# The last rows of w4: from 512-column to 256-column matmuls, smaller last pieces, and a result stored in two halves

## The chip, the cores and the metric

The kernel runs on one core of one Trainium2 chip. The metric is the time of one execution in device microseconds; lower is better. Beside it stands the span, which is the part of the execution that the profiled instructions cover.

## The reference, cut to what matters

One token is decoded by an attention block over a cache of 65,536 keys and, on the same normalised input, by a mixer block; both are added to the input.

```
xn  = layernorm(x)                                     # x: 1 x 1024
q   = (xn @ wq), 32 heads of 128                       # 4 groups of 8 heads share a K and V cache
p   = softmax(q . k_cache / sqrt(128))                 # 65536 keys a group
A   = (p @ v_cache) as one row of 4096 @ wo            # wo: 4096 x 1024
h   = gelu(layernorm(xn) @ w1), shifted along the sequence (length 1)
x1  = xn + h_shifted @ w2
B   = x1 + gelu(layernorm(x1) @ w3) @ w4               # w4: 3584 x 1024
out = x + A + B
```

The sequence has length 1, so the shifted columns of `h` are zeros. All inputs and the output are bf16. The caches are 2 x 4 x 65536 x 128 values, 134 MB, and the weights are another 36 MB.

## The kernel before

Everything is streamed once through three buffers of 64 KB per partition (`slot0` to `slot2`), in the order of the list `stream` (L285): wq, w3, w1 and w2, then a K tile and a V tile for each of eight units (`u`: four groups, two halves of the keys), then wo, then w4. Every load is issued on SyncE's queue by `load` (L288); a buffer's next load is issued by `freed` (L311) when the matmuls that read the buffer are done, so that three loads are in the queue or under way at most. w4 alone is loaded in pieces (`W4_PIECES`, L19): 8, 12, 5, 2 and 1 rows, where a row is what one of the 128 partitions holds for one of 28 steps `c`, 1024 values or 2 KB. Each piece has a semaphore of its own, and the first matmul that reads a piece waits for it.

For each unit, `scores` transposes the K tile in place on VectorE and multiplies it with the queries on TensorE; `maxima`, `weights` and `values` follow. `group_rows` (L509) closes a group and leaves its part of the attention's output, as columns, in `oT`.

The end of the kernel, which the change touches, runs after the last group:

- L540: VectorE computes `o`, the sum of the terms that come from the input row, from `x_halves`. That buffer holds the input row in two halves of 512, on partitions 0 and 32.
- L544 to L550: 32 rows of wo and then the first 20 rows of w4 are multiplied by `row_acc` (L342): two matmuls per row, each 512 columns wide, on two of the four column strips of TensorE. They add up in the PSUM tile `psB`, where the attention's wo product and the w2 product meet. Each such matmul has a weight load of its own.
- L552: VectorE adds `psB` and `o` into `sums` (in the buffer `og`).
- L554: `narrow_rows` multiplies the last `NARROW` = 8 rows of w4 by four matmuls each, 256 columns wide, on all four strips, into the PSUM tiles `pm0` and `pm1`. After the first `AHEAD` = 5 of them, two fp32 matmuls (`mm32`, with the selection matrix `pick`) add `sums` into the same tiles; the 3 remaining rows follow.
- L568 to L571: ScalarE casts `pm0`, VectorE casts `pm1`, each into one half of `out_t` (the buffer of `x_halves`), and ScalarE issues one store of 2 KB, from two partitions, when both casts are done.
- L580 to L587: ScalarE clears the semaphores, and SyncE waits for the store.

The order on each engine is the order in which the program records the operations; `Program.plan` (L124) derives the waits from the regions that they read and write, and TensorE's and SyncE's own instructions are taken to run in order. Since a helper records every operation, most operations carry one of a few line numbers: VectorE, ScalarE and GpSimd have L82, matmuls L106 (weight loads L102), fp32 matmuls L116, loads L89 and stores L93.

Of the kernel before, what the change touches and what calls it, by code (L numbers as in the profile page):

```python
# [14 lines left out]
P = 128  # L15
ROW = 32768
SUBS = 4
SETS = 4
W4_PIECES = (8, 12, 5, 2, 1)  # L19
NARROW = 8  # L20
AHEAD = 5

WIDTH = {F32: 4, BF16: 2}

# [182 lines left out]
def kernel(  # L207
# [14 lines left out]
    nc = tc.nc  # L222
    D = A_x.shape[-1]
# [7 lines left out]
    FC = F // P  # L231
    UKEYS = P * ROW // DH
    assert DH == P and HQ // HKV == 8 and HKV == 4 and D == 1024 and F == 3584 and S == 1
    assert SK == 2 * UKEYS and sum(W4_PIECES) == FC
    NB = 2
# [3 lines left out]
    COLS = (P, 32)  # L239

    prog = Program(nc)
    pe, dve, act, pool = prog, prog.dve, prog.act, prog.pool

    def sb(name, shape, dtype=F32):
        return nc.alloc_sbuf_tensor(name, list(shape), dtype)

    def ps(name, shape):
        return nc.alloc_psum_tensor(name, list(shape), F32)
# [4 lines left out]
    x_row = sb("x_row", [32, D], BF16)  # L253
# [4 lines left out]
    x_halves = sb("x_halves", [64, 512], BF16)  # L258
    qdiag = sb("qdiag", [P, LEAD + 4 * P], BF16)
    g_col = sb("g_col", [P, 1], BF16)  # L260
# [9 lines left out]
    hT = sb("hT", [P, FC], BF16)  # L270
    oT = sb("oT", [P, 32], BF16)
    ol = sb("ol", [P, DH + 1])
    pick = sb("pick", [64, 2, 32])
# [3 lines left out]
    pm = [ps(f"pm{i}", [P, 512]) for i in range(2)]  # L277
# [8 lines left out]
    tiles = {it: slots[i % 3] for i, it in enumerate(stream)}  # L286

    def load(it):  # L288
        t = tiles[it]
        if it == "wq":  # L290
            prog.load("sp", t[:], A_wq.rearrange("(p c) n -> p (c n)", c=DC))
        elif it == "w3":
            prog.load("sp", t[:, 0:DC * F], B_w3.rearrange("(p c) f -> p (c f)", c=DC))
        elif it == "w12":
            prog.load("sp", t[:, 0:DC * D], B_w1.rearrange("(p c) n -> p (c n)", c=DC))
            prog.load("sp", t[:, DC * D:2 * DC * D], B_w2.rearrange("(m c) n -> m (c n)", c=DC))
        elif it == "wo":
            prog.load("sp", t[:], A_wo.rearrange("(p j) n -> p (j n)", p=P))
        elif it == "w4":
            w4_v = B_w4.rearrange("(m c) n -> m c n", c=FC)  # L300
            c0 = 0
            for n in W4_PIECES:
                prog.load("sp", t[:, c0 * D:(c0 + n) * D], w4_v[:, c0:c0 + n, :].rearrange("p c n -> p (c n)"))
                c0 += n
        else:
            kind, i = it
            g, b = divmod(i, NB)
            cache = A_k_cache if kind == "K" else A_v_cache
            prog.load("sp", t[:], cache[0, g, b * UKEYS:(b + 1) * UKEYS, :].rearrange("(p ct) d -> p (ct d)", p=P))

    def freed(it):  # L311

        n = stream.index(it) + 3
        if n < len(stream):
            load(stream[n])

    load("wq")
    opening = len(prog.ops)

    dve.memset(x_row[:], 0.0)  # L320
    prog.load("act", x_row[0:1, :], A_x[0, 0:1, :])
    load("w3")
    load("w12")

# [9 lines left out]
    for b in range(2):  # L334
        pool.tensor_copy(
            out=spread[:, 2 * b:2 * b + 2, :].rearrange("p r (a i) -> p r a i", a=4),
            in_=ident_f[:, 64 * b:64 * b + 64].rearrange("p (i r) -> p r i", r=2).unsqueeze(2).to_broadcast([P, 2, 4, 32]))
    pool.memset(x_halves[:], 0.0)
    pool.memset(qdiag[:], 0.0)
    pool.memset(g_col[:], 0.0)  # L340

    def row_acc(j, lhsT, rhs, start=False):  # L342
        return pe.mm(psB[32 * j:32 * j + 32, :], lhsT.to_broadcast([P, 32]), rhs, start, False, (0, 32 * j), COLS)

    x_t = p_sb[:, 0:DC * 32].rearrange("p (c j) -> p c j", j=32)
    for a in range(4):
        dve.transpose(out=x_t[32 * a:32 * a + 32].rearrange("p c j -> p (c j)"),
                      in_=x_row[:, 256 * a:256 * (a + 1)].rearrange("p (i c) -> p c i", c=DC))
    dve.tensor_copy(out=xT[:], in_=x_t[:, :, 0])

    def layernorm(src, tag):
# [31 lines left out]
                    in_=sel8[:].unsqueeze(1).unsqueeze(3).to_broadcast([P, 4, 8, 4]))  # L383
    dve.tensor_copy(out=pick[:],
                    in_=ident_f[0:64, 0:64].rearrange("p (j r) -> p j r", r=32)[:, :, 0:1].to_broadcast([64, 2, 32]))
    dve.tensor_scalar(out=ln_s1[:], in0=rstd1[:], scalar1=1.0, scalar2=None, op0=ALU.add)
    dve.tensor_tensor(out=ln_s2[:], in0=negmean1[:], in1=rstd1[:], op=ALU.mult)
    for j in range(2):
        dve.tensor_copy(out=x_halves[32 * j:32 * j + 1, :], in_=x_row[0:1, 512 * j:512 * (j + 1)])

    def row_matmul(rep, cols, widths):
        for c in range(DC):
# [37 lines left out]
    def compute_w12():  # L430
        wt = tiles["w12"][:, 0:2 * DC * D].rearrange("p (w c n) -> p w c n", w=2, c=DC)
        for c in range(DC):
            for q in range(2):
                pe.mm(sc[0:32, q, :], xn2_rep[:, c, :], wt[:, 0, c, 512 * q:512 * (q + 1)], c == 0, c == DC - 1,
                      (0, 0), COLS)
        h1 = p_sb[0:32, 0:1024].rearrange("p (q n) -> p q n", q=2)
        act.activation(out=h1, in_=sc[0:32, 0:2, :], func=ACTF.Gelu_apprx_tanh)
        for c in range(DC):
            for j in range(2):
                row_acc(j, g_col[:], wt[:, 1, c, 512 * j:512 * (j + 1)], start=(c == 0))  # L440
        freed("w12")

    W = ROW // SETS
# [80 lines left out]
    compute_wq()  # L524
    compute_w3()
    compute_w12()
    for u in range(NU):
        g, b = divmod(u, NB)
# [11 lines left out]
    o = tiles["w4"][0:64, FC * D:FC * D + D].bitcast(F32)  # L540
    dve.tensor_scalar(out=o, in0=x_halves[:], scalar1=ln_s1[0:64, 0:1], scalar2=ln_s2[0:64, 0:1],
                      op0=ALU.mult, op1=ALU.add)

    for j in range(32):  # L544
        for h in range(2):
            row_acc(h, oT[:, j:j + 1], tiles["wo"][:, D * j + 512 * h:D * j + 512 * (h + 1)])
    wt = tiles["w4"]
    for c in range(FC - NARROW):
        for j in range(2):
            row_acc(j, hT[:, c:c + 1], wt[:, D * c + 512 * j:D * c + 512 * (j + 1)])  # L550
    sums = og[0:64, :]
    dve.tensor_tensor(out=sums, in0=psB[0:64, :], in1=o, op=ALU.add)  # L552

    def narrow_rows(lo, hi, start=False):  # L554
        for c in range(lo, hi):
            for h in range(2):
                for j in range(2):
                    q = 2 * h + j
                    pe.mm(pm[h][32 * q:32 * q + 32, 0:256], hT[:, c:c + 1].to_broadcast([P, 32]),
                          wt[:, D * c + 512 * j + 256 * h:D * c + 512 * j + 256 * (h + 1)], start and c == lo, False,  # L560
                          (0, 32 * q), COLS)

    narrow_rows(FC - NARROW, FC - NARROW + AHEAD, start=True)
    for h in range(2):
        pe.mm32(pm[h][64 * h:64 * h + 64, 0:256], pick[:].rearrange("p j r -> p (j r)"),
                sums[:, 256 * h:256 * (h + 1)], False, False, (0, 64 * h))
    narrow_rows(FC - NARROW + AHEAD, FC)
    out_t = x_halves[:].rearrange("p (h n) -> p h n", h=2)  # L568
    act.copy(out=out_t[:, 0, :], in_=pm[0][0:64, 0:256])
    dve.tensor_copy(out=out_t[:, 1, :], in_=pm[1][64:128, 0:256])  # L570
    store = prog.store("act", out[0, 0, :].rearrange("(j n) -> j n", j=2), out_t[31:33].rearrange("p h n -> p (h n)"))  # L571

    prog.plan()
    with tc.tile_critical(sync_engine=mybir.EngineType.Pool, no_gpsimd_drain=True):
# [1 line left out]
    tc.close()  # L576
    tc.compile()
    prog.emit(opening, len(prog.ops))
    nums = sorted(s.num for s in prog.sems if s is not store.sem)
    nc.scalar.sem_clear(range(nums[0], nums[-1] + 1))  # L580
    nc.sync.add_instruction(mybir.InstEventSemaphore(
        name=nc.get_next_instruction_name(), engine=mybir.EngineType.SP, ins=[], outs=[],
        sync_info=mybir.SyncInfo(
            on_wait=[mybir.SyncWait(sync_type="semaphore", id=store.sem.num, ant_name=store.sem.name,
                                    wait_mode="sem-ge-imm", wait_value=16)],
            on_update=[mybir.SyncUpdate(sync_type="semaphore", id=store.sem.num, ant_name=store.sem.name,
                                        update_mode="sem-sub-imm", update_value=16)])))  # L587

# [1 line left out]
_INS = ['A_x', 'A_k_cache', 'A_v_cache', 'A_wq', 'A_wo', 'B_x', 'B_w1', 'B_w2', 'B_w3', 'B_w4']  # L590
# [26 lines left out]
```

## Time and profile before

| | |
|---|---|
| time, median of 3 runs | 400.46 us (400.43 to 400.66) |
| the profiled execution's own time | 400.43 us |
| its span | 399.1 us |
| TensorE, matmuls | 221.0 us busy (55%), 1360 |
| VectorE | 210.2 us busy (53%), 156 |
| ScalarE | 27.6 us busy (7%), 35 |
| bytes moved | 170.03 MB in 3760 packets, 426 GB/s over the span |

The page of the profile divides the span into 40 slices and gives each engine's busy share in tenths; the line "DMA" is the mean busy share of the core's 16 DMA engines. q1 is the queue of SyncE's loads, q10 that of ScalarE's one load and one store, and q8 and q14 carry instructions. Lines of the timeline give the start, the duration, the engine, the operation (what it writes and what it reads) and how many such operations in a row; the brackets say how long the engine had been idle before, and what ended that. PE is TensorE's matmuls, PEld its weight loads, DVE VectorE, ACT ScalarE, and ACTq or SPq an engine's issue of a transfer. In a view of transfers in a window, packets are counted by their start, and a queue's last figure is the time that its packets took, as a share of 16 DMA engines over that window.

### The profile page before, as it was taken

What the parts mean: (1) busy time and instruction counts of PE and PEld (TensorE: products, weight loads), DVE (VectorE), ACT (ScalarE), POOL (GpSimd) and SP (SyncE); (2) the same over time, 40 slices, a digit from 0 to 9 for tenths busy, and PEclk for the clock granted to TensorE, in tenths of its full rate; (3) what the DMA queues carried; (4) which work ended last, traced back from release to release, by engine and by line L of the source; (5) the groups of instructions that cost most, each with busy time, mean ns of one, the idle gap of its engine ahead of it and who ended that gap; (6) DMA issues with size and microseconds to landing.
All of it is one profiled execution on the core that took longest, in us unless ns stands there. A gap on an engine that the chain in (4) does not pass through costs nothing.

```text
span 399.1 us, 2559 instructions
## 1 busy us (share of the span) xinstructions
PE 221.0 (55%) x1360; PEld 45.5 (11%) x890; DVE 210.2 (53%) x156; ACT 27.6 (7%) x35; POOL 6.2 (2%) x29
## 2 busy tenths in 40 slices
PE   0250970592669246822874387429552946393586
PEld 0210010000201010011001100101010102010233
DVE  0520010975096549643963696359439932793411
ACT  1010030002000200020002000200010010002000
POOL 2000000000000000000000000000000000000000
PEclk9996895697659686968795679678966986597789
DMA  8989999999999999999999999999999999999996
GB/s 342 479 388 417 471 420 427 421 460 466 422 420 427 420 429 427 460 453 427 415 427 420 434 440 447 448 427 420 427 429 434 440 447 435 427 420 427 402 442 256
DMA packets 3760, 170.03 MB, mean 426 GB/s; under 512 B 419, under 2 KB 421, under 8 KB 678
## 3 DMA queue, kind: packets, MB, share of 16 engines
q1 hardware_dynamic: 3744, 169.87, 98.7%
q8 instruction: 9, 0.15, 0.1%
q14 instruction: 1, 0.01, 0.0%
q10 hardware_dynamic: 6, 0.00, 0.0%
HBM read 169.87 MB, written 0.00 MB: 426 GB/s over the span
## 4 chain that ended last, share of the span: by engine, by line
DMA 56%; DVE 21%; PE 17%; another core or an unknown queue 2%; ACT 2%; issue 0%; SPq 0%; POOLq 0%
DMA slot<-in_A_k_cache_dram 42%; DVE slot L82 15%; PE sc L106 12%; DMA slot<-in_B_w_dram 9%; DMA slot<-in_A_wq_dram 5%; PE oacc L106 4%; DVE p_sb L82 2%; DVE mx L82 2%; ACT p_sb L82 2%; PE pm L122 1%; DVE m L82 0%; DVE rep L82 0%; DVE nball L82 0%; DVE x_halves L82 0%
## 5 line engine op out<-in xcount | busy, mean ns | idle before, releaser
L82 DVE STREAM_TRANSPOSE slot<-slot 128x4096 f32<-128x4096 f32 x32 | 139.4, 4411 | 52.4 <-DMA slot<-in_A_k_cache_dram 52.3
L106 PE MATMUL sc<-slot,qdiag 128*128 128x512 bf16 x512 | 128.4, 410 | 69.7 <-DVE slot L82 69.6
L106 PE MATMUL oacc<-slot,p_sb 128*32 128x512 bf16 x512 | 44.9, 528 | 37.5 <-DVE negmg L82 18.8
L82 DVE STREAM_TRANSPOSE p_sb<-p_sb 128x2048 bf16<-128x2048 bf16 (+2 forms) x10 | 20.8, 2085 | 38.9 <-ACT p_sb L82 38.8
L82 DVE TENSOR_REDUCE mx<-sc 128x1 f32<-128x2048 f32 x8 | 18.3, 2292 | 29.7 <-PE sc L106 29.7
L102 PEld LDWEIGHTS <-qdiag 128*128 128x128 bf16 x128 | 13.0, 102 | 180.8 <-issue 180.8
L82 ACT ACTIVATE p_sb<-sc,nball 128x2048 bf16<-128x2048 f32 x8 | 15.7, 1967 | 250.7 <-DVE nball L82 250.7
L102 PEld LDWEIGHTS <-p_sb 128*32 128x32 bf16 x512 | 17.0, 128 | 62.1 <-issue 19.7
L106 PE MATMUL sc<-slot,ln_rep_b 128*32 128x512 bf16 (+1 forms) x80 | 16.2, 827 | 9.4 <-DMA slot<-in_B_w_dram 9.1
L82 DVE SCALAR_TENSOR_TENSOR og<-oacc,wb,og 128x512 f32<-128x512 f32 x4 | 3.0, 750 | 19.1 <-PE oacc L106 19.1
L122 PE MATMUL pm<-ident_f,mx 128*1 128x128 f32 x8 | 2.4, 296 | 19.1 <-DVE mx L82 19.1
L106 PE MATMUL psB<-slot,oT 128*32 128x512 bf16 x64 | 8.8, 443 | 1.3 <-DVE oT L82 1.3
L116 PE MATMUL pm<-ol,selx 128*128 128x129 f32 x8 | 2.3, 370 | 10.6 <-DVE ol L82 10.6
L82 DVE TENSOR_TENSOR og<-psB,slot 64x512 f32<-64x512 f32 x1 | 0.7, 683 | 13.8 <-PE psB L106 13.8
L106 PE MATMUL sc<-slot,ln_rep_a 128*32 128x512 bf16 x64 | 5.4, 512 | 4.5 <-DMA slot<-in_A_wq_dram 4.5
L116 PE MATMUL pm<-ln_rowsum_a,msk 128*128 128x1 f32 x2 | 0.6, 361 | 13.3 <-DVE ln_rowsum_a L82 13.3
L82 POOL COPY qdiag<-qx 32x32 bf16<-32x32 bf16 x16 | 3.2, 203 | 277.2 <-PE sc L106 251.1
L82 DVE STREAM_TRANSPOSE p_sb<-x_row 32x256 bf16<-32x256 bf16 x4 | 2.5, 616 | 7.4 <-DMA x_row<-in_A_x_dram 7.4
L106 PE MATMUL psB<-slot,hT 128*32 128x512 bf16 x40 | 4.7, 379 | 1.0 <-DMA slot<-in_B_w_dram 1.0
L122 PE MATMUL pm<-ident_f,rep 1*128 1x1 f32 x8 | 1.9, 240 | 5.0 <-DVE rep L82 5.0
L82 ACT COPY og<-oacc 128x512 f32<-128x512 f32 x4 | 2.3, 585 | 32.2 <-PE oacc L106 32.2
L102 PEld LDWEIGHTS <-ln_rep_b 128*32 128x32 bf16 x40 | 1.9, 112 | 22.9 <-issue 22.6
(86 smaller groups left out, 61.8 us busy)
## 6 DMA issues: line engine op xcount, KB each, us to landing
slot<-in_B_w_dram SPq DMA_DIRECT2D x1, 7168.0 KB, 37.4
slot<-in_B_w_dram SPq DMA_DIRECT2D x3, 2048.0 KB, 43.2
slot<-in_B_w_dram SPq DMA_DIRECT2D x1, 3072.0 KB, 33.8
slot<-in_B_w_dram SPq DMA_DIRECT2D x1, 1280.0 KB, 33.5
slot<-in_B_w_dram SPq DMA_DIRECT2D x1, 512.0 KB, 34.3
slot<-in_B_w_dram SPq DMA_DIRECT2D x1, 256.0 KB, 34.5
slot<-in_A_k_cache_dram SPq DMA_DIRECT2D x8, 42.1
slot<-in_A_v_cache_dram SPq DMA_DIRECT2D x8, 36.9
```

What stands on the lines that cost most here:

```text
L82: return program.add(Op(engine, lambda: method(*args, **kw), reads, writes, alone=kw.get("accum_out") is not None))
L102: self.add(Op("pe", lambda: pe.ldweights(lhsT, tile_position=pos), [lhsT], []))
L106: return pe.add_instruction(mybir.InstMatmult(name=nc.get_next_instruction_name(), engine=mybir.EngineType.PE, start_tensor_calc=start, st ...
L116: return self.add(Op("pe", lambda: pe.matmul(out, lhsT=lhsT, rhs=rhs, start=start, stop=stop, tile_position=pos, skip_group_check=True), [ ...
L122: return self.add(Op("pe", lambda: pe.transpose(out, in_, identity), [in_, identity], [out]))
```

## The change

1. `W4_PIECES` becomes 8, 12, 6, 1.5 and 0.5 rows. The last piece is the second half (512 of 1024 values) of the last row.
2. `NARROW` becomes 20 and `AHEAD` 12: all rows of w4 from the ninth on are multiplied as four 256-column matmuls, and `sums` is formed after 8 rows of w4 and added after 20.
3. The columns of the result are dealt out anew. Before, a half `h` was columns 256h to 256h+255 of both 512-column halves; now a half `a` is the columns 512a to 512a+511, in two runs `j` of 256. `part` gives the columns of one `j` as two runs of 256 that lie 512 apart, and w2's, wo's and w4's first rows and the input row are read through it.
4. The last two rows are multiplied for the half `a` = 0 first. That half is cast by VectorE and stored from SyncE's queue; then come the two matmuls per row of the half `a` = 1, a cast by ScalarE and a store from ScalarE's queue. Each store has 1 KB.
5. At the end, SyncE tells ScalarE by a semaphore (`issued`) that it has issued its store, before ScalarE clears the semaphores; SyncE waits for both stores.

```diff
-W4_PIECES = (8, 12, 5, 2, 1)
-NARROW = 8
-AHEAD = 5
+W4_PIECES = (8, 12, 6, 1.5, 0.5)
+NARROW = 20
+AHEAD = 12
...
             for n in W4_PIECES:
-                prog.load("sp", t[:, c0 * D:(c0 + n) * D], w4_v[:, c0:c0 + n, :].rearrange("p c n -> p (c n)"))
-                c0 += n
+                x1 = x0 + int(n * D)
+                prog.load("sp", t[:, x0:x1], w4_v[:, x0:x1])
+                x0 = x1
...
+    def part(rows, c, j):
+
+        return rows[:, D * c:D * (c + 1)].rearrange("p (a j n) -> p a j n", a=2, j=2)[:, :, j, :]
...
-                row_acc(j, g_col[:], wt[:, 1, c, 512 * j:512 * (j + 1)], start=(c == 0))
+                row_acc(j, g_col[:], part(wt[:, 1, c, :], 0, j), start=(c == 0))
...
-            row_acc(h, oT[:, j:j + 1], tiles["wo"][:, D * j + 512 * h:D * j + 512 * (h + 1)])
+            row_acc(j, oT[:, c:c + 1], part(tiles["wo"], c, j))
...
-            row_acc(j, hT[:, c:c + 1], wt[:, D * c + 512 * j:D * c + 512 * (j + 1)])
+            row_acc(j, hT[:, c:c + 1], part(wt, c, j))
...
+    def narrow_row(c, a, start=False):
+        for j in range(2):
+            x0 = D * c + 512 * a + 256 * j
+            q = 2 * a + j
+            pe.mm(pm[a][32 * q:32 * q + 32, 0:256], hT[:, c:c + 1].to_broadcast([P, 32]), wt[:, x0:x0 + 256], start, False,
+                  (0, 32 * q), COLS)
+
+    for c in range(FC - NARROW, FC - NARROW + AHEAD):
+        for a in range(2):
+            narrow_row(c, a, start=c == FC - NARROW)
+    for a in range(2):
+        pe.mm32(pm[a][64 * a:64 * a + 64, 0:256], pick[:].rearrange("p j r -> p (j r)"),
+                sums[:, 256 * a:256 * (a + 1)], False, False, (0, 64 * a))
+    for c in range(FC - NARROW + AHEAD, FC - 2):
+        for a in range(2):
+            narrow_row(c, a)
+    out_t = x_halves[:].rearrange("p (a n) -> p a n", a=2)
+    stores = []
+
+    def finish(a, copy, engine):
+        copy(out=out_t[:, a, :], in_=pm[a][64 * a:64 * a + 64, 0:256])
+        stores.append(prog.store(engine, out[0, 0, 512 * a:512 * (a + 1)].rearrange("(j n) -> j n", j=2), out_t[31:33, a, :]))
+
+    narrow_row(FC - 2, 0)
+    narrow_row(FC - 1, 0)
+    finish(0, dve.tensor_copy, "sp")
+    narrow_row(FC - 2, 1)
+    narrow_row(FC - 1, 1)
+    finish(1, act.copy, "act")
...
+    event(nc.sync, mybir.EngineType.SP, update=(issued, 1))
+    event(nc.scalar, mybir.EngineType.Activation, wait=(issued, 1))
+    nums = sorted(x.num for x in prog.sems if all(x is not y.sem for y in stores))
     nc.scalar.sem_clear(range(nums[0], nums[-1] + 1))
...
+    for y in stores:
+        event(nc.sync, mybir.EngineType.SP, wait=(y.sem, 16))
```

More of the change, by code (lines that the diff above doesn't have):

```diff
@@ L299, in load @@
         elif it == "w4":
-            w4_v = B_w4.rearrange("(m c) n -> m c n", c=FC)
-            c0 = 0
+            w4_v = B_w4.rearrange("(m c) n -> m (c n)", c=FC)
+            x0 = 0
             for n in W4_PIECES:
-                prog.load("sp", t[:, c0 * D:(c0 + n) * D], w4_v[:, c0:c0 + n, :].rearrange("p c n -> p (c n)"))
-                c0 += n
+                x1 = x0 + int(n * D)
+                prog.load("sp", t[:, x0:x1], w4_v[:, x0:x1])
+                x0 = x1
         else:
@@ L388 @@
     for j in range(2):
-        dve.tensor_copy(out=x_halves[32 * j:32 * j + 1, :], in_=x_row[0:1, 512 * j:512 * (j + 1)])
+        dve.tensor_copy(out=x_halves[32 * j:32 * j + 1, :].rearrange("o (a n) -> o a n", a=2), in_=part(x_row[0:1, :], 0, j))
     def row_matmul(rep, cols, widths):
@@ L542 @@
                       op0=ALU.mult, op1=ALU.add)
-    for j in range(32):
-        for h in range(2):
-            row_acc(h, oT[:, j:j + 1], tiles["wo"][:, D * j + 512 * h:D * j + 512 * (h + 1)])
+    for c in range(32):
+        for j in range(2):
+            row_acc(j, oT[:, c:c + 1], part(tiles["wo"], c, j))
     wt = tiles["w4"]
@@ L549 @@
         for j in range(2):
-            row_acc(j, hT[:, c:c + 1], wt[:, D * c + 512 * j:D * c + 512 * (j + 1)])
+            row_acc(j, hT[:, c:c + 1], part(wt, c, j))
     sums = og[0:64, :]
     dve.tensor_tensor(out=sums, in0=psB[0:64, :], in1=o, op=ALU.add)
[L554 to L571, printed above, removed]
+    def narrow_row(c, a, start=False):
+        for j in range(2):
+            x0 = D * c + 512 * a + 256 * j
+            q = 2 * a + j
+            pe.mm(pm[a][32 * q:32 * q + 32, 0:256], hT[:, c:c + 1].to_broadcast([P, 32]), wt[:, x0:x0 + 256], start, False,
+                  (0, 32 * q), COLS)
@@ L578, with event @@
     prog.emit(opening, len(prog.ops))
-    nums = sorted(s.num for s in prog.sems if s is not store.sem)
-    nc.scalar.sem_clear(range(nums[0], nums[-1] + 1))
[L581 to L587, printed above, removed]
+    issued = nc.alloc_semaphore("issued")
+    def event(engine, kind, wait=None, update=None):
+        sem, value = wait or update
+        sync = dict(on_wait=[], on_update=[mybir.SyncUpdate(sync_type="semaphore", id=sem.num, ant_name=sem.name,
+                                                update_mode="sem-sub-imm" if wait else "sem-add-imm",
+                                                update_value=value)])
+        if wait:
+            sync["on_wait"] = [mybir.SyncWait(sync_type="semaphore", id=sem.num, ant_name=sem.name,
+                                              wait_mode="sem-ge-imm", wait_value=value)]
+        engine.add_instruction(mybir.InstEventSemaphore(
+            name=nc.get_next_instruction_name(), engine=kind, ins=[], outs=[], sync_info=mybir.SyncInfo(**sync)))
+    event(nc.sync, mybir.EngineType.SP, update=(issued, 1))
+    event(nc.scalar, mybir.EngineType.Activation, wait=(issued, 1))
+    nums = sorted(x.num for x in prog.sems if all(x is not y.sem for y in stores))
+    nc.scalar.sem_clear(range(nums[0], nums[-1] + 1))
+    for y in stores:
+        event(nc.sync, mybir.EngineType.SP, wait=(y.sem, 16))
 _INS = ['A_x', 'A_k_cache', 'A_v_cache', 'A_wq', 'A_wo', 'B_x', 'B_w1', 'B_w2', 'B_w3', 'B_w4']
```

## The prediction

> **What bounds the kernel now.** The page first: is the end set by transfers or by engines?
>
> ```profile
> DMA  8989999999999999999999999999999999999996
> q1 hardware_dynamic: 3744, 169.87, 98.7%
> q8 instruction: 9, 0.15, 0.1%
> ```
>
> The 16 DMA engines work in every slice but the last: the 170 MB of loads on SyncE's queue (q1) are the kernel. A second queue, q8, moved nine packets of 16 KB of program. The chain of waits from 340 us on shows the end:
>
> ```profile
> 362.59 34.50 DMA slot<-in_B_w_dram
> 397.13 0.34 PE pm L106 x4
> 397.49 0.43 DVE x_halves L82
> ```
>
> So w4's last piece sets the end, and 3.3 us lie behind its landing. The timeline of the last stretch shows how each piece is met:
>
> ```profile
> 395.25 0.73 PE L106 MATMUL pm<-slot,hT 128*32 128x256 bf16 x20 [0.34 <-DMA slot<-in_B_w_dram]
> 396.50 0.40 PE L106 MATMUL pm<-slot,hT 128*32 128x256 bf16 x8
> 397.13 0.29 PE L106 MATMUL pm<-slot,hT 128*32 128x256 bf16 x4 [0.23 <-DMA slot<-in_B_w_dram]
> 397.45 0.36 ACT L82 CAST x_halves<-pm 64x256 bf16<-64x256 f32 x1 [26.45 <-PE pm L106]
> 397.49 0.43 DVE L82 CAST x_halves<-pm 64x256 bf16<-64x256 f32 x1 [1.85 <-PE pm L106]
> 397.95 0.26 ACTq L93 DMA_DIRECT2D out_dram<-x_halves  x1
> ```
>
> TensorE waits for the last piece, not the other way round. Then I read the transfers in narrow windows. Each transfer is dealt evenly to the 16 DMA engines, and each engine closes its share with a packet of 4 bytes ("under 512 B" counts these). The window 21.7 to 22.5 holds the end of the first transfer; 357.9 to 358.95 and 358.95 to 360.2 hold that of the last K tile:
>
> ```profile
> DMA packets 32, 0.92 MB, mean 1147 GB/s; under 512 B 16, under 2 KB 16, under 8 KB 16
> DMA packets 16, 0.52 MB, mean 499 GB/s; under 512 B 8, under 2 KB 8, under 8 KB 8
> DMA packets 16, 0.52 MB, mean 419 GB/s; under 512 B 8, under 2 KB 8, under 8 KB 8
> ```
>
> At the start all 16 engines close together; by 358 us eight are late, by one to two microseconds. Up to there eight program fetches had been made (seven on q8, one of 8 KB on q14, at 75.3). Each fetch makes one engine late, each time another one, and as the engines are never idle a late one stays late. For the fetch at 378.46, the share of its window gives 1.06 us for the fetch, and the 16 KB packet behind it on that engine takes 1.12 us, where its neighbours take 0.61: a fetch costs its engine 1.06 + 0.50 = **1.55 us**. The late engines close w4's last piece, and TensorE waits for the last of them.
>
> The ninth fetch, by windows 396.2 to 396.7 (two lines) and 396.44 to 396.47 (three):
>
> ```profile
> DMA packets 34, 0.07 MB, mean 135 GB/s; under 512 B 8, under 2 KB 8, under 8 KB 33
> q8 instruction: 1, 0.02, 13.7%
> DMA packets 2, 0.02 MB, mean 546 GB/s; under 512 B 1, under 2 KB 1, under 8 KB 1
> q8 instruction: 1, 0.02, 228.1%
> q1 hardware_dynamic: 1, 0.00, 1.9%
> ```
>
> Eight engines close last, at 396.3 to 396.7, and the ninth fetch starts in the same 0.03 us in which one of them has closed. Which one? The engine that the first fetch (43.36) hit closes 1.93 us behind the earliest at 69.69 and, followed transfer by transfer, 1.99 us behind it at 379.28, third of the late ones. At 396.3 to 396.44 two close, then this one, then five. So the ninth fetch goes to the engine of the first: q8's fetches go round eight engines. Here it costs nothing, because that engine's loads were just done.
>
> **When a fetch is due.** Busy time by windows from the start; the counts of PE and PEld together are the TensorE instructions so far:
>
> ```profile
> 0.00:39.50 39.50, 8.15 (x76) 3.67 (x45) 9.61 (x35) 3.88 (x6) 3.78 (x17) 0.92 0.96 405
> 0.00:43.36 43.36, 11.79 (x96) 4.04 (x56) 9.61 (x35) 3.88 (x6) 3.78 (x17) 0.88 0.96 408
> 0.00:394.20 394.20, 218.36 (x1320) 44.33 (x852) 209.10 (x154) 27.25 (x34) 6.21 (x29) 0.80 1.00 430
> 0.00:396.46 396.46, 220.28 (x1348) 45.19 (x878) 209.79 (x155) 27.25 (x34) 6.21 (x29) 0.80 1.00 429
> ```
>
> First fetch at 152 instructions, ninth at 2226: 2074 for eight steps, 259 each, which is 16 KB at 63 bytes an instruction. So fetches follow TensorE's place in its program, with a delay. TensorE stood at instruction 121 from before 31 us to 39.5, and the first fetch came at 43.36, so it was due between 121 and 152; eight steps of 256 (16 KB at 64 bytes) on, the ninth was due between 2169 and 2200. Before the change these pass at 394.2 (2172 there) to 395.5, so the fetch started 1.0 to 2.3 us after it was due.
>
> **The change, part by part.**
>
> *Rows 8 to 19 of w4 become four matmuls each* (the 12-row piece, waited for at 392.15). By the order of the two programs TensorE gets 48 instructions more (24 weight loads, 24 matmuls), all behind instruction 2131, the count at 392.1. Their own time: 20 such matmuls took 0.73 us, so 48 take about 1.8, from 392.15 to 393.9, in place of 2.77; the addition of `psB` (0.68) and the four passes of `mm32` (0.65) move ahead of 395 too. The next piece lands near 395.8: worth nothing, covered by the landings; 1.9 us of cover.
>
> But instructions 2169 to 2200 now lie 38 to 69 behind 392.15, at 0.73 us per 40: at 392.8 to 393.4 in place of 394.2 to 395.5. With the same delays the ninth fetch starts at 394.4 to 395.1, perhaps a packet (0.4) later. Its engine closes at 396.46, so the fetch now falls **inside** its loads, with over 0.9 us to spare. Price: 1.55 us on that engine, 396.46 to 398.01. It then closes last, 1.33 us behind the present last (396.68). Bounds: 0 (it comes after the closing, or to an engine with slack) and 1.55; with the fetch alone 1.06, which makes 0.84 late. I take 1.55, since the half microsecond stands behind a fetch among 64 KB packets too (338.9: 2.91 against 2.42).
>
> The Trainium skill says otherwise on the fetch: "Runtime: NRT & Kernel Launch", Instruction fetch mechanics, has crossing a 16 KiB boundary as mostly hidden; by that the time would be rival 1's. For the sequencer the trace agrees (TensorE never waits on it); for the DMA engine it doesn't, 1.55 us each time. The same section gives TensorE's instruction memory 128 KiB, refilled in blocks of 16, so eight blocks; the trace's round of eight fits that.
>
> *Pieces 6, 1.5, 0.5 for 5, 2, 1.* Same bytes, same number of packets (8 per engine and piece). By the trace's packets of 10, 4 and 2 KB (389, 159, 84 ns) the line is 9 ns plus 37.5 per KB; 12, 3 and 1 KB give 461, 122 and 47. Per engine 8 x 632 before, 8 x 630 after: nothing. Between -0.1 and +0.1, the 1 KB packets lying outside the rows.
>
> *Behind the last landing.* Two matmuls in place of four: the casts started 0.32 and 0.36 behind the first of four; after two, 0.31. The last cast is ScalarE's (0.36) in place of VectorE's (0.43), and ScalarE issues its store itself: 0.31 + 0.36 + 0.03 = 0.70 from matmul to store, before 397.95 - 397.13 = 0.82. Gain 0.1. From there to the end 1.15, as before; half the bytes, still two packets. The first half's cast and its store on SyncE run ahead, behind all loads in that queue, with nothing waiting behind them; its landing comes 0.3 us or more before the other. The two event instructions more on SyncE and ScalarE lie beside the store's flight; 0 to +0.1.
>
> *Strided reads* of `wo` and of `w4`'s first rows, and the new order in `x_halves` and w2's sums: same counts and sizes; the scores' matmuls already read strided. `wo` and eight rows end at 391.1, 1.0 us before TensorE is let on at 392.15: that much cover, worth nothing.
>
> **Sum**, against the profiled execution's 400.43 (span 399.1, 1.33 outside): last closing 398.01; TensorE starts 0.45 after the last closing (397.13 - 396.68), at 398.46; store at 399.16; end 400.31; outside 1.33: 401.64. The median is 0.03 above the profiled run: **401.67**, 1.21 up (0.3%).
>
> **Rivals.**
> 1. *The fetch is hidden* (it goes to an unhit engine, closing by 394.7 to 395, or still comes last). Then only the gain stays: 400.46 - 0.1 = 400.35. For it: eight engines have slack of over a microsecond, and the place at 396.46 is that of one fetch only. Against: fetch and closing in 0.03 us, on the engine that eight steps of rotation would name. 0.13.
> 2. *Half the price*: with small packets the half microsecond behind the fetch is absent: 400.46 + (1.06 - 0.22) - 0.1 = 401.2. No row has a fetch amid packets under 16 KB. 0.05.
> 3. *Faster by more*: if the fetch came to rest on no engine and the last piece's landing fell with its size. The 512 KB and 256 KB pieces land 0.45 behind their last bytes alike, and bytes set the rest, so this needs something unseen: 0.02, about 399.6. It decides from 0.8 us less landing on.
> 4. *More than one engine late*, as the fetch also holds up a piece that TensorE then meets too late (24 matmuls of 0.85 us against 1.0 us between landings): up to 0.4 more, 402.0. 0.03.
>
> **How the numbers follow.** A measurement of this kernel tells about 0.2% (0.8 us) from no change. The main case, 0.77, has 401.3 to 401.9 as its own range (price 1.2 to 1.6, the small terms' 0.2). With rival 4 slower has 0.80; rivals 1 and 2 stay inside 0.2%: same 0.18; faster 0.02. The main case alone leaves 0.23 out, so the range reaches down to rival 1: 400.3 to 401.9.
>
> **What would show it.** Right: one q8 fetch near 394.5 to 395.3 and none at 396.46; one engine closing alone, over a microsecond behind the others, near 398.0; the wait for w4's last piece ending near 398.4; two narrow matmuls, ScalarE's cast, its store at 399.2. Wrong: the fetch early but the last closing still near 396.7 (rotation wrong: 400.35), or the fetch still behind the closing. A `wo` phase ending after 392.2 would show a price for strided reads.

## The result, and the profile after

| | before | after |
|---|---|---|
| median | 400.50 us (22 runs, 400.31 to 400.74) | 401.68 us (22 runs, 400.34 to 402.10) |
| ratio after to before | | 1.0021, 95% interval 1.0013 to 1.0029 |
| the profiled execution | 400.43 us, span 399.1 | 400.36 us, span 399.0 |

The executions of the changed kernel stand in two groups with nothing between: 8 at 400.34 to 400.71 (median 400.48) and 14 at 401.55 to 402.10 (median 401.82). Before, all lie within 0.43 us. The median of 401.68 is a place in the upper group; the ratio, which weighs both, is 0.2%. The profile that came with the result is of the lower group; a further run of the same kernel (`e9_after_again` below, 401.97 us) is of the upper one. Both have to be read.

Lower group, timeline of the end:

```profile
392.61 1.68 PE L106 MATMUL pm<-slot,hT 128*32 128x256 bf16 x44
394.22 0.65 PE L116 MATMUL pm<-og,pick 64*64 64x256 f32 x4
395.88 1.55 PE L106 MATMUL pm<-slot,hT 128*32 128x256 bf16 x32 [1.01 <-DMA slot<-in_B_w_dram]
397.47 0.37 ACT L82 CAST x_halves<-pm 64x256 bf16<-64x256 f32 x1 [26.49 <-PE pm L106]
397.87 0.25 ACTq L93 DMA_DIRECT2D out_dram<-x_halves  x1
```

The narrow matmuls and the fp32 matmuls of `mm32` are done a microsecond before the third piece is met at 395.88. The last cast starts at 397.47 and the store at 397.87, 0.08 before the old kernel's.

Upper group, the same stretch:

```profile
396.14 1.33 PE L106 MATMUL pm<-slot,hT 128*32 128x256 bf16 x30 [1.62 <-DMA slot<-in_B_w_dram]
397.51 0.42 DVE L82 CAST x_halves<-pm 64x256 bf16<-64x256 f32 x1 [5.98 <-PE pm L106]
398.67 0.40 PE L106 MATMUL pm<-slot,hT 128*32 128x256 bf16 x2 [1.20 <-DMA slot<-in_B_w_dram]
399.11 0.37 ACT L82 CAST x_halves<-pm 64x256 bf16<-64x256 f32 x1 [27.97 <-PE pm L106]
399.51 0.26 ACTq L93 DMA_DIRECT2D out_dram<-x_halves  x1
```

Up to the first half's cast this execution is 0.25 us behind the lower group's, since its w4 landed that much later as a whole. Then TensorE stands for 1.20 us before the last two matmuls: most of the 1.64 us between the two stores is that wait for the last piece, half a row. The chain of waits says the same; lower group first, then upper:

```profile
362.24 34.54 DMA slot<-in_B_w_dram
396.82 0.62 PE pm L106 x8
```
```profile
362.88 35.75 DMA slot<-in_B_w_dram
398.67 0.41 PE pm L106 x2
```

Where the last piece lost it, the transfers in narrow windows show. Lower group, 396.18 to 396.21; upper group, 396.49 to 396.52; upper group, 396.95 to 398.4:

```profile
DMA packets 4, 0.02 MB, mean 683 GB/s; under 512 B 1, under 2 KB 2, under 8 KB 3
q8 instruction: 1, 0.02, 223.5%
```
```profile
DMA packets 3, 0.02 MB, mean 614 GB/s; under 512 B 0, under 2 KB 2, under 8 KB 2
q8 instruction: 1, 0.02, 230.0%
```
```profile
DMA packets 1, 0.00 MB, mean 0 GB/s; under 512 B 1, under 2 KB 1, under 8 KB 1
```

In the lower group the ninth program fetch starts as an engine closes ("under 512 B 1"), as it did before the change. In the upper group it starts among 1 KB packets with no closing beside it, and after 396.95 exactly one packet is left on all 16 engines, a closing of 4 bytes, which a window of 0.02 us finds at 397.59. The engine had moved all its data; the fetch came between its last data and its closing, and held the closing for 1.1 us. TensorE is let on 1.08 behind that closing, where 0.45 is usual: 0.6 more, close to the half microsecond that the prediction found behind a fetch.

### The profile page after: what moved, and what is told of

The parts are those of the page before. It is cut to its first block, busy times and chain, and to the rows that moved or that the text cites. A ratio compares the mean times of both kernels' runs of the same rounds, so it can differ in the third digit from the quotient of the medians.

```text
span 399.0 us, 2610 instructions
## 1 busy us (share of the span) xinstructions
PE 225.7 (57%) x1384; PEld 46.6 (12%) x914; DVE 210.3 (53%) x156; ACT 27.6 (7%) x35; POOL 6.2 (2%) x29
## 4 chain that ended last, share of the span: by engine, by line
DMA 56%; DVE 21%; PE 17%; another core or an unknown queue 2%; ACT 2%; issue 0%; POOLq 0%; SPq 0%
DMA slot<-in_A_k_cache_dram 42%; DVE slot L82 15%; PE sc L106 13%; DMA slot<-in_B_w_dram 9%; DMA slot<-in_A_wq_dram 5%; PE oacc L106 4%; DVE p_sb L82 2%; DVE mx L82 2%; ACT p_sb L82 2%; PE pm L122 1%; DVE m L82 0%; DVE rep L82 0%; DVE nball L82 0%; PE pm L106 0%
## 5 line engine op out<-in xcount | busy, mean ns | idle before, releaser
L106 PE MATMUL sc<-slot,qdiag 128*128 128x512 bf16 x512 | 130.4, 416 | 66.4 <-DVE slot L82 66.2
L106 PE MATMUL oacc<-slot,p_sb 128*32 128x512 bf16 x512 | 47.0, 548 | 37.5 <-DVE p_sb L82 18.8
L106 PE MATMUL sc<-slot,ln_rep_a 128*32 128x512 bf16 x64 | 6.3, 579 | 4.4 <-DMA slot<-in_A_wq_dram 4.4
```

What stands on the lines that cost most here:

```text
L106: return pe.add_instruction(mybir.InstMatmult(name=nc.get_next_instruction_name(), engine=mybir.EngineType.PE, start_tensor_calc=start, st ...
```

## The experiments

The theory (A): the ninth fetch goes to the DMA engine of the first, and makes the end 1.3 us later if it starts ahead of that engine's closing. The rival (B): the upper group comes from the new tail, its small pieces or its two stores. The first four runs set one against the other.

**e1_wide12**: the changed kernel with the matmuls of the old.

```diff
-NARROW = 20
-AHEAD = 12
+NARROW = 8
+AHEAD = 6
```

> The changed kernel with rows 8 to 19 of w4 left as two 512-column matmuls each (NARROW 8, AHEAD 6); the new pieces, the two stores and the strided reads stay. TensorE has as many instructions as before the change. Theory A (the ninth program fetch goes to the DMA engine of the first, and costs 1.3 us where it gets in ahead of that engine's last packets): the fetch is due as late as before, so every execution is fast, 400.3 to 400.6, with none near 401.7. Theory B (the slow executions of the changed kernel come from its tail: pieces of 3 KB and 1 KB per partition, or the two stores): two groups as in the changed kernel, 400.4 and 401.8, about 6 in 10 in the upper one.

Measured: 11 runs, 400.58 to 401.12, median 400.92 against 400.54 (ratio 1.0009, 1.0000 to 1.0018). There is no upper group, so the pieces and the stores alone don't make one, against B. But it is not 400.4 either, as A had it: 0.4 is lost. The timeline says where:

```profile
396.10 0.84 PE L106 MATMUL pm<-slot,hT 128*32 128x256 bf16 x24 [0.93 <-DMA slot<-in_B_w_dram]
396.87 0.65 PE L116 MATMUL pm<-og,pick 64*64 64x256 f32 x4
397.44 0.41 PE L106 MATMUL pm<-slot,hT 128*32 128x256 bf16 x8
397.94 0.37 ACT L82 CAST x_halves<-pm 64x256 bf16<-64x256 f32 x1 [26.89 <-PE pm L106]
```

With the fp32 matmuls behind the third piece, and that piece a row longer (met at 396.10 in place of 395.25), TensorE works through from 396.10 on and is itself the bound; the last cast starts at 397.94. So the new pieces need the early sum, which the narrow rows bring. In this trace the fetch starts at 397.16, when all engines have closed, and hurts nobody.

**e2_narrow_only**: the kernel before, with the new matmuls alone.

```diff
-NARROW = 8
-AHEAD = 5
+NARROW = 20
+AHEAD = 12
```

> The kernel before with NARROW 20 and AHEAD 12 alone: pieces of 8, 12, 5, 2, 1 rows, one store. Theory A: the 48 instructions that TensorE gets stand where the changed kernel has them, so two groups again, 400.5 and 401.8, or all in the upper one. Theory B: 400.4 to 400.6 throughout, since pieces and store are the old ones.

Measured: 12 runs, 4 at 400.44 to 400.65 and 8 at 401.75 to 402.14 (ratio 1.0023, 1.0013 to 1.0033). The two groups come with the 48 instructions and without pieces or stores. The profile is of the upper group: the fetch at 396.08 among 2 KB packets, and after 396.9 one engine with seven packets left:

```profile
DMA packets 7, 0.01 MB, mean 8 GB/s; under 512 B 1, under 2 KB 1, under 8 KB 7
```

**e3_before_plus48** and **e4_before_plus128**: the old tail; the instructions are added 340 us before the end.

```diff
     compute_w12()
+    for c in range(24):            # e4: 64
+        q = 32 * (c % 4)
+        pe.mm(oacc[q:q + 32, 0:64], xn2_rep[:, c % 8, :], xn_rep[:, 0:2, :].rearrange("p c n -> p (c n)"), True, True,
+              (0, q), COLS)
```

> The kernel before with 24 weight loads and 24 matmuls of 64 columns added behind w2's product, at about 48 us, where TensorE waits for the first K tile; their result is overwritten. The tail is the old one. Theory A: the ninth fetch is due 48 instructions sooner, at 391 to 393.5 us, and gets in ahead of the loads in most executions: 401.6 to 402.1, perhaps a few at 400.5. Theory B: 400.5 as before, since nothing in the tail differs.

> The same with 64 weight loads and 64 matmuls, 128 instructions. Theory A: the ninth fetch is due 128 instructions sooner, near 384 us in wo's product, well ahead of the end of the loads: every execution at 401.6 to 402.1, and in the trace one DMA engine closes alone near 398.0. Theory B, or a ninth fetch that goes to an engine not yet hit: 400.4 to 400.7.

Measured: e3 401.70 to 402.08 in all 5 runs (ratio 1.0034, 1.0022 to 1.0046), e4 401.72 to 403.25 in all 5 (1.0042, 1.0030 to 1.0054). B is out: nothing in the tail differs, and every execution is in the upper group or, twice in e4, above it. In e3 the fetch starts at 395.56, in a window (395.55 to 395.57) without a closing, and one engine is left behind the others; the fetch, then the window 396.7 to 398.4:

```profile
q8 instruction: 1, 0.02, 335.9%
DMA packets 11, 0.02 MB, mean 12 GB/s; under 512 B 2, under 2 KB 2, under 8 KB 11
```

In e4 it starts at 391.40, not soon after 384 as expected. e4's window 396.7 to 398.4 and its last matmuls:

```profile
DMA packets 13, 0.03 MB, mean 17 GB/s; under 512 B 2, under 2 KB 2, under 8 KB 13
```
```profile
398.41 0.29 PE L106 MATMUL pm<-slot,hT 128*32 128x256 bf16 x4 [0.23 <-DMA slot<-in_B_w_dram]
```

Two closings are left there (the last two pieces'), with 11 packets of data; before the change the wait ended at 397.13. Two of e4's runs, 402.51 and 403.25, lie above the group; what they met was not seen.

Now the question was why the changed kernel falls into two groups. TensorE's counts give when the fetch is due. In e1 the fetch met engines that had run empty, and its delay was taken for the shortest; the counts up to 396.05, 396.30 and 397.16:

```profile
0.00:396.05 396.05, 221.35 (x1324) 44.19 (x855) 209.76 (x155) 27.26 (x34) 6.21 (x29) 0.79 1.00 429
0.00:396.30 396.30, 221.56 (x1332) 44.39 (x866) 209.76 (x155) 27.26 (x34) 6.21 (x29) 0.79 1.00 429
0.00:397.16 397.16, 222.42 (x1352) 44.94 (x882) 209.76 (x155) 27.26 (x34) 6.21 (x29) 0.79 0.99 428
```

TensorE stood at 2179 from the end of the 12-row piece to 396.10, when the third piece let it on. If the fetch had been due by then, it should have come when its engine ran empty and not at 397.16; so it was taken to be due between 2179 and the prediction's 2200, which makes the delay in e1 0.85 to 1.05 us. This is an assumption, and e6 below speaks against it: there the fetch was due by the same places and still came after its engine had run empty. The delays that follow are counted from these places. In the lower-group trace of the changed kernel the same counts fall so:

```profile
0.00:393.10 393.10, 222.45 (x1318) 44.58 (x850) 209.28 (x155) 27.24 (x34) 6.21 (x29) 0.78 1.00 430
0.00:393.30 393.30, 222.65 (x1326) 44.77 (x858) 209.48 (x155) 27.24 (x34) 6.21 (x29) 0.78 1.00 430
```

2184 at 393.30, so by these places due at 393.25 to 393.5; the fetch started at 396.20, 2.7 to 3.0 later. By the same counts it started 2.6 to 3.5 after due in e3 and 2.6 to 3.6 in e4. Theory A then has two forms: A1, a busy engine takes the fetch only some 3 us after it is due; A2, at the next packet. Four runs for that.

**e5_narrow14**: the changed kernel, 24 instructions more than before in place of 48.

```diff
-NARROW = 20
-AHEAD = 12
+NARROW = 14
+AHEAD = 6
```

> The changed kernel with NARROW 14 and AHEAD 6: rows 8 to 13 of w4 stay two 512-column matmuls each, rows 14 to 27 are four of 256, and the fp32 matmuls follow row 19, still ahead of the third piece. 24 TensorE instructions more than before the change in place of 48, and the ninth fetch is due when TensorE is at row 14 or 15, near 394 us in place of 393.1. Theory A1 (the fetch costs 1.3 us unless it starts behind the closing of its DMA engine at 396.5, and on a busy engine it starts about 3 us after it is due): it starts at about 397, every execution is fast, 400.3 to 400.6. Theory A2 (it gets in at the next packet, about 1 us after it is due, and the chance of the executions lies elsewhere): two groups, or 401.8 throughout.

Measured: 11 runs, 400.25 to 400.77, median 400.37 against 400.48 (ratio 0.9999, 0.9990 to 1.0007); no upper group. This keeps the pieces, the early sum and the two stores. Its median is the lowest of all the kernels here, and not to be told from that of the kernel before. Its record has eight q8 packets; the ninth is missing, so its start isn't shown.

**e6_after_minus_w1**: the changed kernel without w1's product.

```diff
-        for c in range(DC):
-            for q in range(2):
-                pe.mm(sc[0:32, q, :], xn2_rep[:, c, :], wt[:, 0, c, 512 * q:512 * (q + 1)], c == 0, c == DC - 1,
-                      (0, 0), COLS)
-        h1 = p_sb[0:32, 0:1024].rearrange("p (q n) -> p q n", q=2)
-        act.activation(out=h1, in_=sc[0:32, 0:2, :], func=ACTF.Gelu_apprx_tanh)
```

> The changed kernel without w1's product and its gelu (it leaves out a result that nothing reads): 24 to 26 TensorE instructions fewer at about 45 us, nothing else. The ninth fetch is due that much later in the tail, at 393.5 in place of 393.1. A1: it starts near 396.5, so more executions are fast than the 8 of 22 of the changed kernel, most or all at 400.3 to 400.7. A2: as the changed kernel or slower, 401.8. A rival that puts the two groups down to the tail's pieces and stores: 8 fast of 22 as before.

Measured: 11 runs, 8 at 400.24 to 400.62 and three at 400.83, 400.87 and 401.19; median 400.45. The upper group is gone. In its trace the fetch starts at 396.89, with no loads beside it. By the counts it was due at 393.4 to 393.8 (2184 at 393.50, 2199 at 393.80), 3.1 to 3.5 us before. All engines had closed a quarter of a microsecond before it came; the window 396.62 to 396.88:

```profile
DMA packets 0, 0.00 MB, mean 0 GB/s; under 512 B 0, under 2 KB 0, under 8 KB 0
```

So a long delay isn't a matter of a busy engine alone. The three runs between the groups have no trace, but their spans are on record: 399.0, 398.9 and 399.1 us, as long as those of the eight (398.9 to 399.1). What they lost lies outside the span, not in w4's landing.

**e7_before_plus24**: as e3, with `range(12)`.

> The kernel before with 12 weight loads and 12 matmuls of 64 columns added at about 48 us, 24 instructions; their result is overwritten. The ninth fetch is due in the 12-row piece, near 394.2. A1: it would start at 397.2 if the engine were busy till then, so it starts at the closing, 396.5: every execution as the kernel before, 400.4 to 400.8. A2: it starts near 395.2, inside the loads: 401.6 to 402.1.

Measured: 11 runs, 400.38 to 400.66. The counts put the fetch due at 393.8 to 394.9, over 1.5 us before the closings; taken at the next packet, about 1 us after it was due, it would have cost the full price, in every run. It started at 396.57, beside a closing:

```profile
DMA packets 3, 0.02 MB, mean 820 GB/s; under 512 B 2, under 2 KB 2, under 8 KB 2
q8 instruction: 1, 0.02, 330.6%
```

A2 is out: the fetch came 1.7 to 2.8 us after it was due by the counts, at the closing.

**e8_after_plus24**: the changed kernel with the same addition.

> The changed kernel with the same 24 instructions added at about 48 us. The ninth fetch is due near 392.6 in place of 393.1. A1: it starts at 395.6, ahead of the closing: every execution, or nearly, in the upper group, 401.5 to 402.1. If the fetch had nothing to do with the two groups: 8 fast of 22.

Measured: 12 runs, 3 at 400.16 to 400.52 and 9 at 401.72 to 402.20. That is not "every execution", and 9 of 12 can't be told from the 14 of 22 without the addition, so this run decides nothing between A1 and a chance that has nothing to do with the fetch. It ran on the same chip as e5 to e7 and has both groups, so that those three have no upper group is not the chip's doing. In its trace, of the lower group, the fetch was due at 392.65 to 392.9 and started at 396.32, 3.4 to 3.7 later, beside a closing.

**e9_after_again** and **e10_after_again**: the changed kernel unaltered.

> The changed kernel itself, one look. Its executions fall into two groups, 400.3 to 400.7 (8 of 22) and 401.6 to 402.1 (14 of 22), and the trace at hand is of the first. If this one is of the second: A1 wants the ninth fetch to start ahead of the closing of its DMA engine (by 396.2), that engine to close alone near 398.0, and the wait for w4's last piece to end near 398.4. If it is of the first, the fetch starts at or behind the closing.

> The changed kernel itself, a second look, for the same question and with the same expectations as the look before: upper group, a ninth fetch by 396.2 and one engine closing alone near 398.0; lower group, the fetch at or behind the closing.

Measured: 401.97 (upper; its lines stand above) and 400.53 (lower; the fetch at 396.54 beside a closing). The order is as expected, ahead of the closing in the upper one and behind it in the lower. Of the times, three in the upper one are not: the fetch starts at 396.50, not by 396.2, since that execution's w4 landed 0.3 us later as a whole; its engine closes alone at 397.59, not near 398.0; the wait ends at 398.67, not near 398.4.

## Why the prediction was right or wrong

**The bound and the mechanism: right.** The end is w4's last landing; a program fetch makes one DMA engine late; the ninth falls on an engine already late; 48 more TensorE instructions can bring it forward into the loads. e3 shows this with nothing else changed. Rival 1 (hidden), in its form "still comes last", is what the lower group does: 8 of 22 executions.

**The price: right in size.** The sum had 401.67; the upper group is 401.82. Its two terms were 1.33 late and 0.1 gained. In e9 the other engines had closed by 396.94, so TensorE would have been let on at about 397.39; it was let on at 398.67, 1.28 late. That is 0.21 behind the predicted 398.46, because w4 landed later as a whole. A second part was lacking in the sum: the granted clock was 0.50 in the window 398.0 to 399.2, behind the idle 1.2 us (1.00 at 397.1 to 397.5 before the change), and the last cast started 0.44 behind the matmul, not 0.31.

**When the fetch starts: wrong.** The step is "With the same delays the ninth fetch starts at 394.4 to 395.1 ... with over 0.9 us to spare". TensorE passed the places 2169 to 2200 when the prediction said (392.9 to 393.5 in the traces of the two groups, predicted 392.8 to 393.4); that the fetch is due exactly there is not shown. The delay of 1.0 to 2.3 us was what failed. It was taken from one fetch, the ninth before the change, whose engine was just running empty. From 2179 to 2200 it measured 2.6 to 3.7 (the changed kernel, e2, e3, e4, e8), so the changed kernel's fetch starts at 396.2 to 396.5, where its engine closes, and not over 0.9 us ahead. The trace before the change could have warned: by the same steps of 256, the third fetch was due at 142.3 to 143.3 and started at 148.14, the eighth at 374.1 to 375.2 and started at 378.46. Nothing was to spare: some executions pay and some don't, and the lower group shows what the prediction itself named as a sign of being wrong, a fetch still behind the closing. The forecast of one outcome at 0.77 was a forecast of the larger group; that the median falls there is luck as far as the prediction goes, owed to 14 of 22. The range of 400.3 to 401.9 holds the median, but half of its width (400.71 to 401.55) lies where no execution does.

**Edits costed at nothing: right, but for one link between them.** The 64 matmuls of wo's product take 8.77 us with the strided reads (e9) as without (before, e2), at a granted clock of 0.84 between 380 and 391 us; where the clock is 0.70 to 0.72, they take 9.5 with them (lower group) as without (e7). So the late end of this phase in the lower group's trace, near 393, is the clock's and no price of strided reads, and the landings hide it. The early sum has a microsecond of cover in the lower group's timeline. Its worth, put at nothing, is 0.4 us as soon as the third piece has six rows (e1): the two edits hang together, which the prediction did not see.

**Behind the last landing: right.** In the lower group's trace the store starts 0.72 us behind the last two matmuls (their weight load at 397.15), forecast 0.70, and at 397.87 against 397.95. The lower group's median is 0.02 below the old one, and e5's 0.11, neither of which a measurement can tell from none.

**Hidden or not.** The Trainium skill's "mostly hidden" ("Runtime: NRT & Kernel Launch", Instruction fetch mechanics) fits TensorE in the timelines above, where its waits end with a landing, and does not fit the load that the fetch delays: every execution of e3 ends 1.2 to 1.5 us later for it.

## What to carry to other kernels

Where transfers bound a kernel to its end, count the program fetches as transfers: each one delayed one DMA engine for good here, and a change that only adds instructions can move those behind it. If one lands near the last closing, the times come in two groups; look at every run before a median, and take a profile of each group. Fewer instructions ahead of the end (here 14 narrow rows in place of 20) left no execution of 11 in the upper group.

## What the runs showed of the hardware

- A 16 KB fetch held its DMA engine for 1.0 to 1.1 us (1.06 at 378.46, 1.10 in e9), and what came next on that engine was about 0.5 us late (1.12 against 0.61 us behind the fetch at 378.46); even a 4-byte closing, with all data moved, was late by 1.1 us and landed 0.6 us later still (e9).
- Counted from the places 2179 to 2200, the ninth fetch started 2.6 to 3.7 us later while loads were under way (the changed kernel, e2, e3, e4, e8; 1.7 to 2.8 in e7), and 0.85 to 1.05 us later on empty engines in e1, but 3.1 to 3.5 us later in e6, where the engines had run empty too. What sets this delay, and whether these are the places at which the fetch is due, stays open; it was about as long in e4, where the fetch came 5 us before the end of the loads, as in the changed kernel.
- In the traces that were followed closing by closing for it (before, both groups of the changed kernel, e8), the ninth fetch goes to the engine that the first had made late.
